# Transposing the memory part into the probability tile and adding it on VectorE, with four smaller edits, in an attention-and-experts kernel

## The chip, the cores and the metric

The kernel runs on one core of one Trainium2 chip. The metric is the device time of one execution in microseconds. All arithmetic is float32 or a split of it.

## The reference

Three layers in a row; only the first is touched, and the last copy of the third.

```python
# B, H, S, D = 4, 8, 576, 64
scores = (q @ k.T) / sqrt(D);  causal mask;  a = softmax(scores);  local = a @ v
phi(x) = where(x > 0, x, exp(x) - 1) + 1
mem_out = (phi(q) @ M_prev) / (phi(q) @ z_prev + 1e-6)
g = sigmoid(beta)
x = g * mem_out + (1 - g) * local          # to (2304, 512)
x = square(relu(x @ w_in)) @ w_out         # d_ff 2048
# then 8 experts, top 2 of them for each token, each relu(x @ w1[e]) @ w2[e], gated and summed
```

## The kernel before

The attention stage works on 16 pairs of heads. Of a pair, both heads lie side by side on the 128 partitions (64 each). The 576 tokens of a pair are four units of queries, `u` = 0 to 3: unit 0 holds two row tiles of 128 queries, units 1 and 2 one each, unit 3 the tail of 64. So there are 64 steps `t`, one for each unit, and the program is written out by hand in a fixed order; each engine takes its instructions in that order. The loop of step `t` issues, for TensorE: `scores(t + 3)` (the products of query and key into one of two double banks, L323 or L353, and the mask, L330), `av(t - 1)` (the products of probabilities and values into bank 7, L412), then `transp(t)` (probabilities turned through banks 4 and 5, L377, L385, L387). VectorE takes the row minimum of `scores(t + 3)` (L334) and copies bank 5 to SBUF (L382, L388); ScalarE makes the exponentials (L339, L358), copies bank 4 (L380, L386) and copies bank 7 into the tile `xT` that the next layer reads (L93, in `put_x`); GpSimd scales the probabilities (L349, L364).

The memory part of a pair is made one pair ahead by `phi_part`: exp of the raw queries on ScalarE (L279), minimum with 1 and a fused maximum-and-add on VectorE (L284, L285), two batches of products with M and z into bank 6 (L291), and a division (L294 to L296) that leaves `mem[n]`, tokens on the partitions, five row tiles. `av` then adds it to the local part inside TensorE: it multiplies the rows of `mem` with an identity into the same bank 7 (L417), two products (one for each head) for each row tile.

`scaled` makes -0.125 times the queries of a pair on ScalarE (L270), into a tile `qs` that the score products read. It is placed by `later(step, ...)`, which runs pieces at the end of a step; so are the four pieces of `phi_part` and the conversion of the first weights of the next layer (`convert`, one part about every four steps, L249 to L258). Copies of activations between two layers (`split_x`) stand in steps 39 to 60.

Everything behind the attention stage (the two dense layers, the routing, the eight experts) is unchanged but for `evac`, which copies an expert's result out of a bank with the gate as a scale (L781 on ScalarE for even tiles, L783 on VectorE for odd ones) and starts an indirect DMA that adds it to the output (L784).

## Time and profile before

| what | value |
|---|---|
| median of 3 runs (lowest, highest) | 1119.62 us (1117.81, 1119.9) |
| the profiled execution's own time | 1117.35 us |
| its span, first to last instruction | 1115.6 us |
| TensorE busy | 1094.4 us, 98% |
| VectorE, ScalarE, GpSimd busy | 591.4, 512.4, 239.0 us |
| attention stage | from the start to about 231 us |

The attention stage is the first fifth of the span. Times in the rows are microseconds from the span's start; an engine's mean is for one instruction in ns. PE is TensorE, PEld its weight loads, DVE VectorE, ACT ScalarE, POOL GpSimd. A float32 product is two records in the trace (two passes), a transposition one.

### The profile page before, as it was taken

The page shows a single profiled execution, that of the slowest core. Times are in us where ns is not written, and L with a number is a line of the kernel's source. Part 1 is how long each engine was busy: PE and PEld are TensorE (multiplying, and loading weights), DVE is VectorE, ACT ScalarE, POOL GpSimd, SP SyncE. Part 2 cuts the span into 40 slices and gives each one's busy share as a digit, 9 for nine tenths or more (in the row PEclk, how much of TensorE's full clock was granted, in tenths as well). Part 3 has the DMA queues.
Part 4 walks back from the last instruction along what each step waited for, and adds up shares of the span by engine and source line. Part 5 has one row for each costly group of instructions (what it writes and reads, how often), then busy time and mean ns, then how long its engine had stood idle before and what let it go on. Part 6 is the DMA issues. An engine that isn't in the chain of part 4 may idle for free. (4 is left out here: it accounts for less than half of the span.)

```text
span 1115.6 us, 19030 instructions
## 1 busy us (share of the span) xinstructions
PE 1094.4 (98%) x7182; PEld 955.5 (86%) x7182; DVE 591.4 (53%) x1484; ACT 512.4 (46%) x1202; POOL 239.0 (21%) x357
## 2 busy tenths in 40 slices
PE   8999999999999999999999999999999999999996
PEld 6777777789999888998988989899999999999995
DVE  6788777669995445434347545444444444342211
ACT  5777777667665334334245533433333333331211
POOL 5566666600000022200202012102020202020202
PEclk9999999999999999999999999999999999999998
DMA  6996532034330011100115508536353545442113
GB/s 193 279 275 212 168 100 86 18 106 126 119 118 19 2 57 57 48 10 11 58 52 153 175 20 225 161 100 147 98 133 105 130 113 125 121 87 37 24 23 46
DMA packets 98278, 115.47 MB, mean 104 GB/s; under 512 B 9984, under 2 KB 67328, under 8 KB 98176
## 3 DMA queue, kind: packets, MB, share of 16 engines
q1 hardware_dynamic: 89664, 94.42, 28.1%
q0 software_dynamic: 8512, 19.74, 8.7%
q8 instruction: 58, 0.95, 0.4%
q14 instruction: 44, 0.36, 0.1%
HBM read 77.80 MB, written 36.33 MB: 102 GB/s over the span
## 5 line engine op out<-in xcount | busy, mean ns | idle before, releaser
L472 PE MATMUL bk<-xsplit,u 128*128 128x384 f32 x1152 | 219.8, 338 | 0.0
L564 PE MATMUL bk<-u,hsplit 128*128 128x512 f32 x864 | 215.2, 393 | 0.0
L773 PE MATMUL bk<-u,hsplit 128*128 128x512 f32 x802 | 213.8, 391 | 0.0
L472 PEld LDWEIGHTS bk<-xsplit,u 128*128 128x128 f32 x1152 | 202.5, 188 | 9.4 <-issue 3.1
L564 PEld LDWEIGHTS bk<-u,hsplit 128*128 128x128 f32 x864 | 160.7, 188 | 29.3
L773 PEld LDWEIGHTS bk<-u,hsplit 128*128 128x128 f32 x802 | 147.3, 188 | 27.0
L764 ACT ACTIVATE hsplit<-bk 128x312 fp32r<-128x312 f32 (+2 forms) x126 | 54.3, 431 | 180.6 <-PE bk L760 180.6
L760 PE MATMUL bk<-xsplit,u 128*128 128x312 f32 (+1 forms) x864 | 134.7, 311 | 1.9 <-ACTq L925 1.9
L760 PEld LDWEIGHTS bk<-xsplit,u 128*128 128x128 f32 x864 | 128.4, 188 | 4.7 <-ACTq L925 2.3
L695 POOL DMA_INDIRECT xs<-x,si x36 | 38.3, 1064 | 410.3 <-DVE runs L688 173.4
L483 ACT ACTIVATE hact<-bk 128x384 f32<-128x384 f32 x96 | 46.6, 486 | 141.1 <-PE bk L472 141.1
L596 DVE TENSOR_TENSOR u<-xT,u 128x512 fp32r<-128x512 f32 x89 | 60.9, 691 | 86.7 <-ACT u L595 85.6
L784 POOL DMA_INDIRECT out_dram<-xT,tk x30 | 47.6, 1587 | 270.1 <-ACT xT L781 263.4
L488 DVE TENSOR_TENSOR hact<-hact 128x384 f32<-128x384 f32 x64 | 35.7, 558 | 124.4 <-ACT hsplit L484 124.4
L595 ACT ACTIVATE u<-xT 128x512 fp32r<-128x512 f32 x89 | 55.6, 628 | 88.6 <-PE bk L773 81.0
L760 PE MATMUL bk<-x2b,u 128*128 128x312 f32 x576 | 87.7, 308 | 0.0
L760 PEld LDWEIGHTS bk<-x2b,u 128*128 128x128 f32 x576 | 83.3, 189 | 0.6
L349 POOL TENSOR_SCALAR P<-P,sm,omg 128x128 f32<-128x128 f32 (+3 forms) x126 | 76.2, 617 | 31.7 <-DVE rd L294 27.8
L765 DVE SCALAR_TENSOR_TENSOR hsplit<-bk,hsplit 128x312 fp32r<-128x312 f32 (+2 forms) x68 | 33.0, 487 | 87.3 <-ACT hsplit L764 87.3
L339 ACT ACTIVATE P<-bk,mx 128x128 f32<-128x128 f32 (+3 forms) x128 | 66.0, 528 | 12.9 <-DVE mx L334 12.7
L412 PE MATMUL bk<-PT,vr 128*64 128x128 f32 (+2 forms) x896 | 59.8, 269 | 0.6 <-ACT PT L380 0.3
L765 DVE SCALAR_TENSOR_TENSOR xsplit<-bk,hsplit 128x312 fp32r<-128x312 f32 (+1 forms) x58 | 27.7, 477 | 60.0 <-ACT hsplit L764 59.5
(188 smaller groups left out, 1464.6 us busy)
## 6 DMA issues: line engine op xcount, KB each, us to landing
xT<-in_moe_w_dram SPq DMA_DIRECT2D x89, 256.0 KB, 3.2
cst<-in_moe_w_in_dram SPq DMA_DIRECT2D x32, 256.0 KB, 2.8
cst<-in_moe_w_out_dram SPq DMA_DIRECT2D x32, 256.0 KB, 2.9
xs<-zero SPq DMA_DIRECT2D x5, 1536.0 KB, 10.7
out_dram<-zero SPq DMA_DIRECT2D x4, 1472.0 KB, 7.4
qr<-in_q_dram SPq DMA_DIRECT2D x16, 352.0 KB, 3.1
xr<-xs SPq DMA_DIRECT2D x7, 774.0 KB, 5.0
vr<-in_v_dram SPq DMA_DIRECT2D x16, 320.0 KB, 3.6
```

What stands on the lines that cost most here:

```text
L339: nc.scalar.activation(pb[:, j * 512 + o:j * 512 + o + w], sp[:, j, o:o + w], AF.Exp, bias=mx[:, x:x + 1], scale=-1.0, accum_out=sm[:, x:x ...
L349: (nc.gpsimd if t or j else nc.vector).tensor_scalar(v, v, sm[:, x:x + 1], omg[:, h0 + j:h0 + j + 1], op0=ALU.mult, op1=ALU.mult)
L412: nc.tensor.matmul(o[j * D:(j + 1) * D, a:e], vv[:k_, c, j, :], pt[:k_, j * step + x:j * step + x + e - a], start=i == 0, stop=False, skip ...
L472: nc.tensor.matmul(hb, l[:, sl], r, start=cc == 0 and n == 0, stop=cc == NCC - 1 and n == 2)
L564: nc.tensor.matmul(bank[y0 + t], l[:, sl], r, start=fc == 0 and n == 0, stop=fc == NFC - 1 and n == 2)
L595: nc.scalar.activation(hi, st, AF.Copy)
L596: eng.tensor_sub(lo, st, hi.bitcast(F32))
L760: nc.tensor.matmul(bank[bk][:, :n_], l[:, cs], r[:, cc, sl], start=cc == 0 and n == 0, stop=cc == NCC - 1 and n == 2)
L764: nc.scalar.activation(hh[:, sl], bank[bk][:, :n_], AF.Relu)
L765: nc.vector.scalar_tensor_tensor(hl[:, sl], bank[bk][:, :n_], 0.0, hh[:, sl].bitcast(F32), op0=ALU.max, op1=ALU.subtract)
L773: nc.tensor.matmul(bank[self.ybank + t], l[:, sl], r, start=fc == 0 and n == 0, stop=fc == NFE - 1 and n == 2)
L784: add = nc.gpsimd.indirect_dma_start(out=out, out_offset=bass.IndirectOffsetOnAxis(ap=self.tok[:n, t:t + 1], axis=0), in_=y, in_offset=Non ...
```

## The change

- The memory part of a row tile is no longer multiplied into bank 7. In `transp` of units 0, 1 and 3 the tile of `mem` is turned by TensorE (one transposition of 128 x 128) into the free columns of the banks that hold the turned probabilities, and comes to SBUF with the copies of these banks, which grow from 384 to 512 columns (for unit 3 from 128 to 256). Unit 1 turns the tiles of units 1 and 2. `put_x` then makes one VectorE addition of bank 7 and that tile, in place of ScalarE's copy. The very first unit (`t` = 0) keeps the old way. The tiles `PT` get three buffers in place of two.
- ScalarE copies bank 5 as well in units 2 and 3, which VectorE did.
- Features: for all pairs but the first, relu(-x) and exp(-that) on ScalarE in place of exp on ScalarE and a minimum on VectorE. In the first pair the minimum stands ahead of the exponential.
- `scaled` runs one step earlier.
- Eight identity products into bank 7 stand between the second and third score products of the program.
- The last copy of the last expert is cut in halves of 256 columns, the first on ScalarE, the second on VectorE.

```diff
--- before.py
+++ after.py
@@ -85,12 +85,17 @@
         return [xsplit[:, (2 * i + j) * NCC * w:(2 * i + j + 1) * NCC * w].rearrange("p (c t) -> p c t", c=NCC)
                 for j in range(2)]
 
-    def put_x(hp, t0, src):
+    def put_x(hp, t0, src, more=None):
+
         n = src.shape[-1]
         while n:
             g, o = divmod(t0, G)
             w = min(n, G - o)
-            nc.scalar.activation(xT[g][:, hp, o:o + w], src[:, :w], AF.Copy)
+            if more is None:
+                nc.scalar.activation(xT[g][:, hp, o:o + w], src[:, :w], AF.Copy)
+            else:
+                nc.vector.tensor_add(xT[g][:, hp, o:o + w], src[:, :w], more[:, :w])
+                more = more[:, w:]
             src, t0, n = src[:, w:], t0 + w, n - w
 
     NE = w1.shape[0]
@@ -276,12 +281,16 @@
         ph = ap2.tile([P, S], F32, name="phi", bufs=2)
         mg = ap2.tile([P, MW], F32, name="mg", bufs=1)
         mem[n] = ap2.tile([P, NB, P], F32, name="mem")
-        nc.scalar.activation(e, qq, AF.Exp)
+        if n:
+            nc.scalar.activation(e, qq, AF.Relu, scale=-1.0)
+            nc.scalar.activation(e, e, AF.Exp, scale=-1.0)
+        else:
+            nc.vector.tensor_scalar_min(e, qq, 0.0)
+            nc.scalar.activation(e, e, AF.Exp)
         nc.gpsimd.tensor_scalar(mg[:, :P], mr_[n % 2][:, :P], gtc[:, n % (H // 2):n % (H // 2) + 1], 1.0,
                                 op0=ALU.mult, op1=ALU.mult)
         nc.gpsimd.tensor_copy(mg[:, P:], mr_[n % 2][:, P:])
         yield
-        nc.vector.tensor_scalar_min(e, e, 1.0)
         nc.vector.scalar_tensor_tensor(ph, qq, 0.0, e, op0=ALU.max, op1=ALU.add)
         yield
         for ts in ((0, 1, 2), (3, 4)):
@@ -364,28 +373,39 @@
             nc.gpsimd.tensor_scalar(pb[:, :S], pb[:, :S], sm[:, :1], omgc[:, h0 // 2:h0 // 2 + 1],
                                     op0=ALU.mult, op1=ALU.mult)
 
+    apart = {}
+
     def transp(t):
         n, u = units[t]
         pb = PB.pop(t)
-        pt = ap3.tile([P, 2 * 512], F32, name="PT", bufs=2)
+        pt = ap3.tile([P, 2 * 512], F32, name="PT", bufs=3)
         PT[t] = pt
         if u < NK - 1:
-            m = sum(w for _, w, _ in tiles(u))
+            turn = t and u < 2
+            m = sum(w for _, w, _ in tiles(u)) + (P if turn else 0)
             blocks = [(0, 0), (1, 1), (2, 2)] if u == 0 else [(c, c) for c in range(u + 2)]
             for j in range(2):
                 for c, x in blocks:
                     nc.tensor.transpose(bank[4 + j][:, x * P:(x + 1) * P], pb[:, j * 512 + c * P:j * 512 + (c + 1) * P], ident)
+                if turn:
+                    nc.tensor.transpose(bank[4 + j][:, 3 * P:], mem[n][:, 2 * u + j, :], ident)
                 dst = pt[:, j * 512:j * 512 + m]
-                if j == 0:
-                    nc.scalar.activation(dst, bank[4][:, :m], AF.Copy)
+                if j == 0 or u == 2:
+                    nc.scalar.activation(dst, bank[4 + j][:, :m], AF.Copy)
                 else:
                     nc.vector.tensor_copy(dst, bank[5][:, :m])
+            if turn:
+                apart[t] = [pt[:, (4 * j + 3) * P:(4 * j + 4) * P] for j in range(2)]
+                if u:
+                    apart[t + 1] = apart[t][1:]
         else:
             for c in range(4):
                 nc.tensor.transpose(bank[4][:, c * P:(c + 1) * P], pb[:, c * P:(c + 1) * P], ident)
             nc.scalar.activation(pt[:, :512], bank[4], AF.Copy)
             nc.tensor.transpose(bank[5][:, :P], pb[:, 4 * P:], ident)
-            nc.vector.tensor_copy(pt[:, 512:512 + P], bank[5][:, :P])
+            nc.tensor.transpose(bank[5][:, P:2 * P], mem[n][:, NB - 1, :], ident)
+            nc.scalar.activation(pt[:, 512:512 + 2 * P], bank[5][:, :2 * P], AF.Copy)
+            apart[t] = [pt[:, 512 + 2 * P - TAIL:512 + 2 * P]]
 
     def av(t):
         n, u = units[t]
@@ -396,27 +416,31 @@
         if u == 0:
             w = 2 * P
             work = [(0, P, 0, 0, w), (1, P, w, P, w)]
-            rows = [(0, 0), (1, P)]
+            rows = [(0, 0), (1, P)] if not t else []
         elif u < NK - 1:
             w = P
             work = [(c, P, c * P, 0, w) for c in range(u + 2)]
-            rows = [(u + 1, 0)]
+            rows = []
         else:
             w = TAIL
             work = [(c, P, c * P, 0, w) for c in range(NB)]
-            rows = [(u + 1, 0)]
+            rows = []
         o = bank[7][:, :w]
         step = TAIL if u == NK - 1 else 512
         for i, (c, k_, x, a, e) in enumerate(work):
             for j in range(2):
                 nc.tensor.matmul(o[j * D:(j + 1) * D, a:e], vv[:k_, c, j, :], pt[:k_, j * step + x:j * step + x + e - a],
-                                 start=i == 0, stop=False, skip_group_check=True)
+                                 start=i == 0, stop=i + 1 == len(work) and not rows, skip_group_check=True)
         for i, (qi, a) in enumerate(rows):
             k_ = min(P, w)
             for j in range(2):
                 nc.tensor.matmul(o[j * D:(j + 1) * D, a:a + k_], mem[n][:, qi, j * D:(j + 1) * D], ident[:, P - k_:],
                                  start=False, stop=i + 1 == len(rows), skip_group_check=True)
-        put_x(hp, b * S + q0, o)
+        if rows:
+            put_x(hp, b * S + q0, o)
+        else:
+            for i, more in enumerate(apart.pop(t)[:len(tiles(u)) if u < NK - 1 else 1]):
+                put_x(hp, b * S + q0 + i * P, o[:, i * P:min(w, (i + 1) * P)], more)
 
     NU = len(units)
     CONV0, CONVR, CONVM = 3, 4.1, 1.9
@@ -430,7 +454,7 @@
         yield
 
     for m in range(1, NPAIR):
-        later(NK * (m - 1) - 1, first(m))
+        later(NK * (m - 1) - 2, first(m))
         gen = phi_part(m)
         for k_ in range(4):
             later(NK * (m - 1) + k_, gen)
@@ -496,8 +520,11 @@
     gates()
     sg = {t: scores(t) for t in range(LEAD)}
     phi0 = phi_part(0)
-    for x in (sg[0], sg[0], sg[1], sg[1], sg[0], sg[0], sg[0], sg[1], sg[2], sg[1], phi0, sg[2], sg[1], phi0, sg[2]):
+    for i, x in enumerate((sg[0], sg[0], sg[1], sg[1], sg[0], sg[0], sg[0], sg[1], sg[2], sg[1], phi0, sg[2], sg[1], phi0, sg[2])):
         next(x, None)
+        if i == 2:
+            for _ in range(8):
+                nc.tensor.matmul(bank[7][:, :P], ident, ident, start=True, stop=True)
     transp(0)
     run_late(-1)
     ahead_of = {}
@@ -777,7 +804,11 @@
             for t in tiles[:self.nt]:
                 n = min(P, WIDE - (self.t0 + t) * P)
                 y = ytile()[:n, :]
-                if t % 2 == 0:
+                if self.e == NE - 1 and t == NT2 - 1:
+                    h = DM // 2
+                    nc.scalar.activation(y[:, :h], bank[self.ybank + t][:n, :h], AF.Copy, scale=self.gate[:n, t:t + 1])
+                    nc.vector.tensor_scalar_mul(y[:, h:], bank[self.ybank + t][:n, h:], self.gate[:n, t:t + 1])
+                elif t % 2 == 0:
                     nc.scalar.activation(y, bank[self.ybank + t][:n, :], AF.Copy, scale=self.gate[:n, t:t + 1])
                 else:
                     nc.vector.tensor_scalar_mul(y, bank[self.ybank + t][:n, :], self.gate[:n, t:t + 1])
```

On TensorE, at the end of a pair (`av` of unit 3 of one pair, `transp` of unit 0 of the next; `bk_64` is bank 7, `bk_61` and `bk_62` are banks 4 and 5, `vr` the values, `ident` the identity). Before:

```order
L412 MATMUL bk_64<-PT,vr_142 64x64 [waits Activation_49]
L412 MATMUL bk_64<-PT,vr_142 64x64 x7
L412 MATMUL bk_64<-PT,vr_142 64x64 [waits DVE_49]
L412 MATMUL bk_64<-PT,vr_142 64x64
L417 MATMUL bk_64<-ident,mem 64x64 x2
L377 MATMUL bk_61<-ident,P 128x128 [waits Pool_49] x2
L377 MATMUL bk_61<-ident,P 128x128
L377 MATMUL bk_62<-ident,P 128x128
L377 MATMUL bk_62<-ident,P 128x128 [waits Pool_49]
```

and now:

```order
L432 MATMUL bk_64<-PT,vr_142 64x64 [waits DVE_49,Activation_49]
L432 MATMUL bk_64<-PT,vr_142 64x64 x7
L432 MATMUL bk_64<-PT,vr_142 64x64 [waits Activation_49]
L432 MATMUL bk_64<-PT,vr_142 64x64
L389 MATMUL bk_61<-ident,P 128x128 [waits Pool_49] x2
L389 MATMUL bk_61<-ident,P 128x128
L391 MATMUL bk_61<-ident,mem 128x128
L389 MATMUL bk_62<-ident,P 128x128
L389 MATMUL bk_62<-ident,P 128x128 [waits Pool_49]
L389 MATMUL bk_62<-ident,P 128x128
L391 MATMUL bk_62<-ident,mem 128x128
```

The two products of `mem` ahead of the transpositions are gone, two transpositions of `mem` stand among the others, and the first product of `av` waits for VectorE as well as for ScalarE.

On VectorE, from the row minima of a unit 0 to the division of the next pair's memory part (`mx` are the minima, `sm` the sums, `rd` the divisors). Before:

```order
L334 TENSOR_REDUCE mx<-bk_68 128x2 [waits PE_49]
L334 TENSOR_REDUCE mx<-bk_68 128x2
L382 COPY PT<-bk_62 128x384 [waits PE_49]
L362 RECIPROCAL sm<-sm 128x1 [waits Pool_49]
L284 TENSOR_SCALAR phe<-phe 128x576 [waits Activation_49]
L285 SCALAR_TENSOR_TENSOR phi<-qr_138,phe 128x576 [waits DMAHW7_49,DVE_49]
L334 TENSOR_REDUCE mx<-bk_69 128x2 [waits PE_49]
L382 COPY PT<-bk_62 128x512 [waits PE_49]
L343 RECIPROCAL sm<-sm 128x4 [waits Pool_49]
L294 TENSOR_SCALAR rd<-bk_63 128x6 [waits PE_49]
L295 RECIPROCAL rd<-rd 128x6 [waits DVE_49]
L296 TENSOR_TENSOR mem<-bk_63,rd 128x384 [waits DVE_49]
```

and now:

```order
L343 TENSOR_REDUCE mx<-bk_68 128x2 [waits PE_49]
L343 TENSOR_REDUCE mx<-bk_68 128x2
L97 TENSOR_TENSOR xT_90<-bk_64,PT 128x128 [waits PE_49,Activation_49]
L97 TENSOR_TENSOR xT_90<-bk_64,PT 128x64 [waits DVE_49]
L97 TENSOR_TENSOR xT_91<-bk_64,PT 128x64
L396 COPY PT<-bk_62 128x512 [waits PE_49]
L371 RECIPROCAL sm<-sm 128x1 [waits Pool_49]
L294 SCALAR_TENSOR_TENSOR phi<-qr_138,phe 128x576 [waits DMAHW7_49,Activation_49]
L343 TENSOR_REDUCE mx<-bk_69 128x2 [waits PE_49]
L97 TENSOR_TENSOR xT_91<-bk_64,PT 128x128 [waits PE_49,Activation_49]
L352 RECIPROCAL sm<-sm 128x4 [waits Pool_49]
L303 TENSOR_SCALAR rd<-bk_63 128x6 [waits PE_49]
```

The minimum on `phe` and a copy of 512 columns went away, additions into `xT` came in behind the minima `mx`, and the first copy is wider. The additions' tiles of 64 are pieces of a tile that crosses the border of an `xT` tile.

On ScalarE, around the scaling of the queries of that same pair. Before:

```order
L339 ACTIVATE P,sm<-bk_69,mx 128x384 [waits DVE_49,Pool_49]
L339 ACTIVATE P,sm<-bk_69,mx 128x384
L93 ACTIVATE xT_93<-bk_64 128x128 [waits PE_49]
L386 ACTIVATE PT<-bk_61 128x512 [waits PE_49,Activation_49]
L339 ACTIVATE P,sm<-bk_68,mx 128x512 [waits DVE_49,Pool_49]
L339 ACTIVATE P,sm<-bk_68,mx 128x512
L270 ACTIVATE qs<-qr_138 128x704 [waits DMAHW5_49]
L93 ACTIVATE xT_93<-bk_64 128x64 [waits PE_49]
L380 ACTIVATE PT<-bk_61 128x384 [waits PE_49,Activation_49]
```

and now:

```order
L348 ACTIVATE P,sm<-bk_69,mx 128x384 [waits DVE_49,Pool_49]
L348 ACTIVATE P,sm<-bk_69,mx 128x384
L275 ACTIVATE qs<-qr_138 128x704 [waits DMAHW5_49]
L404 ACTIVATE PT<-bk_61 128x512 [waits PE_49]
L407 ACTIVATE PT<-bk_62 128x256 [waits PE_49]
L348 ACTIVATE P,sm<-bk_68,mx 128x512 [waits DVE_49,Pool_49]
L348 ACTIVATE P,sm<-bk_68,mx 128x512
L394 ACTIVATE PT<-bk_61 128x512 [waits PE_49,Activation_49]
L367 ACTIVATE Pt_156,sm<-bk_69,mx 128x576 [waits DVE_49,Pool_49]
```

The scaling moved from behind the exponentials of unit 2 to ahead of the copies of the tail's transpositions, the copies into `xT` are gone, and the copy of bank 5 (256 columns) is new.

## Rows read from the trace of the kernel before

**Rows 1.** The page: busy time, share of the span and instructions of each engine

```profile
PE 1094.4 (98%) x7182; PEld 955.5 (86%) x7182; DVE 591.4 (53%) x1484; ACT 512.4 (46%) x1202; POOL 239.0 (21%) x357
```

**Rows 2.** Windows: length, busy time of each engine, granted clock, DMA share, GB/s

```profile
24.00:225.00 201.00, 196.59 (x2141) 149.48 (x2140) 155.49 (x366) 144.30 (x441) 124.09 (x244) 1.00 0.54 164
...
111.25:124.63 13.38, 13.07 (x144) 9.94 (x144) 10.92 (x26) 9.97 (x33) 7.96 (x17) 1.00 0.66 222
```

**Rows 3.** Waits of TensorE, 20 to 235 us: total, times, longest of one

```profile
PE bk L323 <- ACT qs L270: 2.5, 8, 0.3
```

**Rows 4.** Timeline of TensorE: three of the 16 starts of a tail's score products

```profile
54.61 1.13 PE L353 MATMUL bk<-kr,qs 128*128 128x288 f32 x4
...
161.66 1.14 PE L353 MATMUL bk<-kr,qs 128*128 128x288 f32 x4
...
216.63 1.13 PE L353 MATMUL bk<-kr,qs 128*128 128x288 f32 x4
```

**Rows 5.** Timeline of TensorE inside one pair

```profile
111.25 0.93 PE L323 MATMUL bk<-kr,qs 64*128 64x128 f32 x8 [0.31 <-ACT qs L270]
...
113.03 0.61 PE L417 MATMUL bk<-ident,mem 128*64 128x128 f32 x8
113.57 0.88 PE L377 MATMUL bk<-ident,P 128*128 128x128 f32 x6
114.37 0.92 PE L323 MATMUL bk<-kr,qs 64*128 64x384 f32 x4
...
116.35 1.09 PE L377 MATMUL bk<-ident,P 128*128 128x128 f32 x8
117.28 0.83 PE L291 MATMUL bk<-mg,phi 128*128 128x130 f32 x6
```

**Rows 6.** Instructions by line and shape, 0 to 400 us: busy, mean ns, idle

```profile
L417 PEld LDWEIGHTS bk<-ident,mem 128*64 128x64 f32 x320 | 20.1, 137 | 0.0
L382 DVE COPY PT<-bk 128x384 f32<-128x384 f32 x32 | 17.8, 555 | 20.1 <-PE bk L377 20.1
L279 ACT ACTIVATE phe<-qr 128x576 f32<-128x576 f32 x16 | 11.1, 692 | 0.0
L382 DVE COPY PT<-bk 128x512 f32<-128x512 f32 x16 | 10.9, 679 | 3.0 <-PE bk L377 2.8
L296 DVE TENSOR_TENSOR mem<-bk,rd 128x384 f32<-128x384 f32 x16 | 8.9, 557 | 0.5
L284 DVE TENSOR_SCALAR phe<-phe 128x576 f32<-128x576 f32 x16 | 7.1, 447 | 0.0
L296 DVE TENSOR_TENSOR mem<-bk,rd 128x256 f32<-128x256 f32 x16 | 6.8, 424 | 0.6
L388 DVE COPY PT<-bk 128x128 f32<-128x128 f32 x16 | 4.6, 285 | 3.1 <-PE bk L387 3.1
```

**Rows 7.** VectorE's window in one pair, then TensorE's timeline

```profile
115.02:122.40 7.38, 7.17 (x16) 1.00 0.62 210
...
122.60 0.80 PE L412 MATMUL bk<-PT,vr 128*64 128x64 f32 x20
```

**Rows 8.** The start: timeline of TensorE, and a window as in group 2

```profile
9.92 1.26 PE L323 MATMUL bk<-kr,qs 64*128 64x512 f32 x4 [1.92 <-ACT P L339]
...
16.84 0.71 PE L291 MATMUL bk<-mg,phi 128*128 128x130 f32 x4 [1.07 <-DVE mem L296]
...
11.96:16.80 4.84, 3.54 (x16) 2.60 (x14) 4.74 (x10) 3.44 (x9) 2.27 (x5) 0.77 0.33 111
11.00:14.00 3.00, 3.00 (x15) 2.47 (x12) 2.24 (x5) 1.28 (x4) 2.82 (x7) 0.50 0.85 292
```

**Rows 9.** The end: timeline

```profile
1095.31 0.43 ACT L764 ACTIVATE xr<-bk 128x312 fp32r<-128x312 f32 x1 [1.29 <-PE bk L760]
...
1095.77 0.48 DVE L765 SCALAR_TENSOR_TENSOR xr<-bk,xr 128x312 fp32r<-128x312 f32 x1 [1.24 <-ACT xr L764]
...
1105.59 0.69 ACT L781 ACTIVATE xT<-bk,gk 112x512 f32<-112x512 f32 x1 [3.45 <-PE bk L773]
```

## The prediction

> **What bounds the kernel now.** I read the busy times first: TensorE works 98% of the span and the next engine 53% [rows 1]. Only an edit that shortens TensorE's stream, or a wait in it, moves the end. Nearly all edits lie in the attention stage, so I then read that stage by windows: from 24 to 225 us TensorE is busy 196.59 of 201 us at a granted clock of 1.00, that is its upper level of 2.4 GHz, while VectorE has 155.49, ScalarE 144.30 and GpSimd 124.09 [rows 2]. In one pair of heads the numbers are 13.07 of 13.38 us for TensorE, 10.92 for VectorE, 9.97 for ScalarE [rows 2]. So TensorE sets the pace, VectorE has 2.5 us a pair to spare and ScalarE 3.4. The pace is a regular one: a tail's score products start at 54.61 and, eight pairs later, at 161.66, which is 13.38 us a pair; from there to 216.63, four pairs with copies for the next layer among them, it is 13.74 [rows 4]. The waits of TensorE name one repeated loss: the scaled queries come late 8 times, 2.5 us in all [rows 3], 0.31 us in the pair shown [rows 5].
>
> **The memory part.** What goes is two products for each of 80 row tiles (5 in each of 16 pairs), except the two tiles of the very first unit. From the weight loads, 320 records keep TensorE's load side busy 20.1 us [rows 6], 1.26 us a pair. By starts, the eight records of a unit 0 take 113.57 - 113.03 = 0.54 us [rows 5], and part of that is a hand-over to the transpositions, which stays when `av` stands right ahead of them. No row shows it alone. At 0.063 a record it is 0.04; from the transpositions, six of which take 0.80 and would stream in 0.70 at the 0.116 that eight take (0.93 / 8) [rows 5], it is 0.10. The 20 records of a pair take 1.35 at the rate of the 0.54, less four hand-overs 0.95 to 1.19. I take 1.05 us a pair as gone, with 0.95 and 1.26 as ends. What comes is five transpositions a pair, 0.065 us each by the difference of eight and six (0.13 for two), 0.116 by the mean; I take the middle, 0.09, so 0.47 a pair (0.33 to 0.58), since they stand inside groups that have their hand-over already. The net is 1.05 - 0.47 = 0.58 us a pair (0.37 to 0.93), and for 78 of 80 tiles, 15.5 pairs, **-9.0 us** (-5.7 to -14.4).
>
> A transposition is also a question of the clock. The pair in the rows has 20 of them among its products and its granted clock is 1.00 [rows 2]. The Trainium skill says ("TensorE: Matmul & The Clock Gate", Part 4: PE-mode transpose) that a transposition does not count as activity of TensorE as a product does, which speaks against exchanging the one for the other. By the row the sum keeps its -9.0; by the rule the clock could fall, and that is the last of the rivals below.
>
> **The work that moves to VectorE and ScalarE.** The additions into `xT` are new. By the built order there are 54 of 128 columns and 32 of 64. The nearest rows are VectorE's division, which also takes one operand from PSUM and one from SBUF: 557 ns for 384 columns and 424 for 256 [rows 6], so 133 ns for 128 columns, and by the same line 291 ns for 128 and 225 for 64. That is 22.9 us, 1.43 a pair. The wider copies cost 2 x (0.679 - 0.555) = 0.25 [rows 6]. What VectorE loses is the minimum, 0.447, the copy of unit 2, 0.679, and that of unit 3, 0.285 [rows 6]. Sum: 10.92 + 1.43 + 0.25 - 1.41 = 11.2 us a pair. ScalarE gets a second pass over 576 elements, 0.69 [rows 6], and two copies that cost VectorE 0.68 and, at 256 columns, at most 0.56 [rows 6], and 0.25 for wider ones: 9.97 + 2.18 = 12.15 at most, with its copies into `xT` not yet taken off. TensorE's new pair is 13.38 - 0.58 - 0.31 = 12.5. So neither becomes the bound by its sum, but VectorE's slack shrinks from 2.5 to 1.3 us.
>
> With that the new wait counts: the first product of `av` now waits for the addition of the unit before, since both use bank 7. Behind `av` on TensorE stand the transpositions, and all copies wait for these. The addition that is latest is that of unit 2, since ahead of it on VectorE stand the division, a part of the weight conversion and a row minimum of 1024 columns. Before, this stretch runs from 115.02 to 122.40 nearly without a gap, 7.17 us busy, and the next `av` starts at 122.60 [rows 7]. The change takes a minimum (0.447) and a copy (0.679) out and puts two additions (0.58) in, so the stretch shortens by 0.55, and TensorE comes to that `av` about 0.5 earlier. It is a tie, on which I put 0.1 us in each of the 12 pairs that hold a conversion (12 parts, one about every four steps): **+1.0 us**, with 0 and 6 as ends (half a microsecond a pair).
>
> **The scaled queries.** One step earlier, a quarter of 13.38 us, they stand behind the exponentials of unit 1. The tile `qr` has been loaded four steps before even then, and SP's order does not change. The 2.5 us go [rows 3]; next late is the copy of bank 4, which `av` needs only after the score products. **-2.5 us**, with 0 as the other end.
>
> **Passes in the first pause.** TensorE waits 1.92 us until 9.92 for the exponentials that free a bank [rows 8], and right behind, from 11 to 14 us, the granted clock is 0.50, the lower level of 1.2 GHz [rows 8]. Eight identity products, 16 records at the 0.116 us of a transposition, are 1.9 us and just fill the pause; at the lower level they end 1.9 us late. But what the start waits for is VectorE: from 11.96 to 16.80 it is busy 4.74 of 4.84 us, and TensorE's second batch waits 1.07 us for it until 16.84 [rows 8]. The minimum of the first pair only changes places inside that stretch. A faster TensorE gives nothing back there: **0**, from -1.5 (the three microseconds at half pace) to +1.0.
>
> **The last copy.** It starts at 1105.59 and takes 0.69 us [rows 9]. Halves would give 0.26 if both engines read the bank at once, but in the built order VectorE's half waits for ScalarE's. How two such steps run in turn the rows show: 0.43 us on ScalarE, and VectorE starts 0.46 after it and needs 0.48 [rows 9], both for 312 columns; in all 0.94, so 256 columns take some 0.84 by the same shares. **+0.15 us** (-0.26 to +0.25). The Trainium skill gives a reason for such an order ("PSUM — Partial Sum Buffer", PSUM bank collisions raise a hardware error): two engines must not access one bank at once on the same partitions. By it the halves cost 0.15, without it they would give 0.26.
>
> **The sum**, against the profiled execution's own 1117.35 us (1.75 more than its span): -9.0 + 1.0 - 2.5 + 0 + 0.15 = -10.35, so 1107.0. That execution lies 2.3 us under the median of the three runs, 1119.62, and under the lowest, 1117.81. The middle of all four is 1118.7, and from there the change gives about **1108.5 us**.
>
> **Rivals.**
> - *VectorE late at bank 7*, faster but by half. If an addition costs 0.2 us more than by the division's rows, or the stretch of rows 7 keeps its 7.4 us, `av` waits 0.4 to 0.5 in the pairs with a conversion or a copy for the next layer, 15 of them, some 6 us: 1114. For it: the tie above. Against it: the stretch loses more than it gains. 0.17.
> - *More goes than the sum has.* The four last pairs take 0.36 us more each than the regular 13.38 [rows 4]; if a shorter stream and a VectorE without the minimum end these waits too, and the net of the memory part is 0.93, the gain is 14.4 + 2.5 + 1.4: 1101. 0.08.
> - *It is absorbed.* The change does less than it says: TensorE's shorter stream only waits for GpSimd's scaled probabilities, whose order and work stay. Then 1118. Against it: GpSimd is busy 7.96 of 13.38 us [rows 2]. 0.07.
> - *Slower by the additions.* Each `av` waits for an addition behind whatever VectorE still has to do. It decides where the wait passes what TensorE saves, 0.58 + 0.16 (2.5 us over 16) = 0.74 us a pair. With VectorE's sum at 13.8, which an addition of 0.8 us in place of 0.29 would make of it, the pair is 0.4 longer than before: 16 x 0.4, 1125. Against it: no row prices such an operation above 0.56. 0.05.
> - *Slower by the clock.* If the stage's clock fell as at the start, three microseconds at half pace cost 1.5 [rows 8]; one such fall in each pair costs 24 and leaves 1132, and seven falls eat the gain. The rule on transpositions above is the reason it could. Against it: 201 us at 1.00 with 20 transpositions a pair [rows 2]. 0.03.
>
> The forecast itself, 1104.5 to 1112.5, has 0.60. A measurement of this kernel tells about 0.2%, 2.2 us, from no change. Faster is forecast, first and second rival: 0.85; same the third: 0.07; slower the last two: 0.08. The range for 8 in 10 runs from 1102.5 (most of the second rival left out) to 1116.
>
> **What would show it.** The products of `mem` shrink to the first unit's 8 records, and 78 transpositions of `mem` are new; the starts of the tail's products come every 12.4 to 12.7 us; the wait for `qs` is gone; additions of 128 columns take 0.27 to 0.32 us; VectorE is busy some 11.2 us a pair. Wrong would be: a wait of `av` for `xT` among TensorE's longest, above 0.4 us a pair; ScalarE's copies of banks 4 and 5 as what TensorE waits for; a granted clock under 1.00 between 24 and 220 us; or a start that moves by more than 1.5 us.

## Result, and the profile after

The changed kernel takes 1109.49 us (median of four runs, 1108.93 to 1109.99) against 1118.82 (four runs, 1117.81 to 1119.9): a ratio of 0.9917, interval 0.9906 to 0.9929, 9.3 us faster. Its profiled execution took 1109.9 us, 7.45 less than that of before. The page's busy line, as in [rows 1]:

```profile
PE 1090.3 (98%) x6964; PEld 951.2 (86%) x6964; DVE 584.5 (53%) x1524; ACT 521.1 (47%) x1178; POOL 239.5 (22%) x357
```

Windows as in [rows 2], the second one regular pair:

```profile
24.00:218.00 194.00, 192.90 (x1944) 145.75 (x1941) 150.39 (x407) 154.92 (x423) 126.25 (x249) 1.00 0.58 172
92.20:104.76 12.56, 12.56 (x132) 9.48 (x130) 10.33 (x29) 10.56 (x30) 8.07 (x16) 1.00 0.70 222
```

A regular pair is 12.56 us where it was 13.38, TensorE fills it wholly, and the clock stays at 1.00 with 30 transpositions in it. VectorE's share is smaller than before, not larger. All waits of TensorE from 20 to 235 us, as in [rows 3]:

```profile
PE bk L432 <- issue: 0.4, 1, 0.4
PE bk L432 <- ACT PT L394: 0.3, 1, 0.3
PE bk L332 <- DMA kr<-in_k_dram: 0.2, 1, 0.2
```

The wait for `qs` is gone, and no `av` waits for an addition. The new and changed instructions, by line and shape as in [rows 6]; the fused operation of the features (L294) took 1153 ns before at the same shape:

```profile
L391 PEld LDWEIGHTS bk<-ident,mem 128*128 128x128 f32 x62 | 8.8, 141 | 0.0
L396 DVE COPY PT<-bk 128x512 f32<-128x512 f32 x31 | 21.4, 690 | 11.6 <-PE bk L391 11.6
L97 DVE TENSOR_TENSOR xT<-bk,PT 128x128 f32<-128x128 f32 x54 | 14.6, 281 | 2.1 <-PE bk L432 1.7 <-ACT phe L286 0.3
L97 DVE TENSOR_TENSOR xT<-bk,PT 128x64 f32<-128x64 f32 x32 | 6.2, 214 | 0.1
L294 DVE SCALAR_TENSOR_TENSOR phi<-qr,phe 128x576 f32<-128x576 f32 x16 | 12.3, 767 | 0.0
L285 ACT ACTIVATE phe<-qr 128x576 f32<-128x576 f32 x15 | 10.2, 681 | 0.0
```

The starts of the tail's score products, one for each pair as in [rows 4]: the second of 16 before, then the second, the twelfth and the last after.

```profile
27.73 1.14 PE L353 MATMUL bk<-kr,qs 128*128 128x288 f32 x4
```

```profile
29.15 1.13 PE L362 MATMUL bk<-kr,qs 128*128 128x288 f32 x4
...
155.04 1.13 PE L362 MATMUL bk<-kr,qs 128*128 128x288 f32 x4
...
207.93 1.13 PE L362 MATMUL bk<-kr,qs 128*128 128x288 f32 x4
```

They give an account of the stage:

| us | first tail | second tail | next ten pairs | last four pairs |
|---|---|---|---|---|
| before | 12.65 | 27.73 | 133.93 | 54.97 |
| after | 11.95 | 29.15 | 125.89 | 52.89 |

So the 14 pairs behind the second tail give 10.12 us, and the start, though 0.70 earlier at the first tail, is 1.42 late at the second. At the end the last copy loses 0.3. In this execution the clock also fell to 0.50 for some 3 us at the branch behind the first expert (near 703 us). That cost it some 1.2 us: from TensorE's first product behind the branch to the end it took 405.55 us, and 404.36 in e1, which is the same kernel without that fall. e1 and e2 show no fall there, e3 and e4 show one, so it is the execution's and not the change's.

### The profile page after: what moved, and what is told of

The parts are those of the page before. It is cut to its first block, busy times and chain, and to the rows that moved or that the text cites. A ratio compares the mean times of both kernels' runs of the same rounds, so it can differ in the third digit from the quotient of the medians.

```text
span 1108.2 us, 18671 instructions
## 1 busy us (share of the span) xinstructions
PE 1090.3 (98%) x6964; PEld 951.2 (86%) x6964; DVE 584.5 (53%) x1524; ACT 521.1 (47%) x1178; POOL 239.5 (22%) x357
```

## Experiments

All are edits of the changed kernel. "Tail" is the start of the second tail's products, "pair" a regular pair (the commonest of the first nine), "14 pairs" from the second tail to the last; these three are from the profiled execution, the rest from all runs.

| kernel | median us (lowest to highest, runs) | ratio to before, interval | tail | pair | 14 pairs |
|---|---|---|---|---|---|
| after | 1109.49 (1108.93-1109.99, 4) | 0.9917, 0.9906-0.9929 | 29.15 | 12.56 | 178.78 |
| e1 again | 1111.21 (1108.03-1111.52, 5) | 0.9917, 0.9901-0.9932 | 30.60 | 12.56 | 179.00 |
| e2 no passes | 1107.11 (1106.39-1109.31, 4) | 0.9889, 0.9873-0.9905 | 28.00 | 12.56 | 179.10 |
| e3 more passes | 1108.36 (1107.19-1108.62, 4) | 0.9895, 0.988-0.991 | 27.61 | 12.56 | 178.57 |
| e4 whole copy | 1109.68 (1108.36-1111.37, 4) | 0.9908, 0.9893-0.9924 | 29.08 | 12.56 | 178.82 |
| e5 memory apart | 1113.39 (1112.18-1114.63, 6) | 0.9948, 0.9936-0.9961 | 27.79 | 13.00 | 183.89 |
| e6 queries late | 1108.39 (1107.4-1109.93, 5) | 0.991, 0.9897-0.9923 | 27.17 | 12.65 | 179.43 |
| e7 features back | 1112.45 (1110.0-1113.67, 6) | 0.9939, 0.9925-0.9952 | 29.40 | 12.73 | 182.56 |
| e8 copy on VectorE | 1110.6 (1108.06-1112.37, 6) | 0.992, 0.9904-0.9935 | 28.45 | 12.72 | 180.62 |
| e9 queries and features | 1113.64 (1112.01-1115.44, 6) | 0.9946, 0.9931-0.9961 | 29.60 | 12.89 | 183.73 |
| e10 more passes, whole copy | 1106.45 (1106.15-1106.76, 4) | 0.9882, 0.9865-0.9899 | 27.61 | 12.56 | 178.46 |
| e11 no passes, whole copy | 1108.46 (1106.2-1109.34, 5) | 0.9898, 0.9881-0.9915 | 27.62 | 12.56 | 178.74 |
| e12 features and copy | 1119.41 (1117.03-1120.62, 11) | 1.0004, 0.9995-1.0013 | 28.07 | 13.31 | 188.31 |

Runs e1 to e4, e5 to e8, e9 to e11 and e12 were made together, each set beside runs of the kernel before. A start differs from one execution to the next by more than most edits do, so the pair and the 14 pairs are what tells the edits of the pair apart.

### The start and the end: e1 to e4

e1 is the changed kernel itself.

> The changed kernel itself, run beside the next three on one chip, as their yardstick: 0.9917 of the kernel before (1109.5 us), tails of the attention stage every 12.56 us from the third pair on, second tail at 29.15 us.

e2 takes the identity products out.

```diff
-        if i == 2:
-            for _ in range(8):
-                nc.tensor.matmul(bank[7][:, :P], ident, ident, start=True, stop=True)
```

> The changed kernel without the eight identity products in the first pause. My theory: they hold the clock up from 11 to 14 us, where TensorE waits for VectorE anyway, and TensorE then idles from 13.1 to 16.8 us, so that the half pace comes from 16.8 to 21 us, where TensorE sets the pace. Without them the half pace is back at 11 to 14 us, the second tail starts at 27.5 to 28.0 us in place of 29.15, and the kernel is 1.2 to 1.7 us faster than the changed one. The rival, that the late start has another cause (the minimum ahead of the exponential, or the old-style first unit): the second tail stays within 0.3 us of 29.15 or comes later, 0 to 1.5 us slower.

e3 adds passes in the next two gaps, ahead of the first and the second batch of memory products of the first pair.

```diff
+            for _ in range(7):
+                nc.tensor.matmul(bank[7][:, :P], ident, ident, start=True, stop=True)
...
+            for _ in range(4):
+                nc.tensor.matmul(bank[7][:, :P], ident, ident, start=True, stop=True)
```

> The changed kernel with seven more identity products ahead of the first batch of memory products of the first pair and four more ahead of the second batch, so that TensorE is hardly idle between 13 and 16.8 us. My theory (the half pace is what costs): the granted clock stays at 1.00 from 16 to 21 us, the second tail starts 1.2 to 2.0 us before 29.15, and the kernel is 1.0 to 2.0 us faster than the changed one. The rival, that the start is bound by VectorE and ScalarE to the first transpositions of unit 1: same within 0.4 us.

e4 leaves the last copy whole, on ScalarE.

```diff
-                if self.e == NE - 1 and t == NT2 - 1:
...
-                elif t % 2 == 0:
+                if t % 2 == 0:
```

> The changed kernel with its last copy whole on ScalarE. My theory: the halves run one behind the other because they read one bank, 0.98 us in all against 0.69, so the whole copy is 0.3 us faster, and the last indirect DMA starts 0.3 us sooner after the start of the last copy. The rival: the halves cost nothing, same within 0.1 us at that place.

The end first: the last copy and the scatter behind it, in the timeline of the changed kernel and then of e4.

```profile
1098.20 0.47 ACT L809 ACTIVATE xT<-bk,gk 112x256 f32<-112x256 f32 x1 [3.45 <-PE bk L800]
1098.70 0.48 DVE L810 TENSOR_SCALAR xT<-bk,gk 112x256 f32<-112x256 f32 x1 [1.85 <-ACT xT L809]
1099.47 1.48 POOL L815 DMA_INDIRECT out_dram<-xT,tk  x1 [0.79 <-DVE xT L810]
```

```profile
1098.19 0.69 ACT L808 ACTIVATE xT<-bk,gk 112x512 f32<-112x512 f32 x1 [3.45 <-PE bk L800]
1099.15 1.48 POOL L811 DMA_INDIRECT out_dram<-xT,tk  x1 [0.48 <-ACT xT L808]
```

From its start to the scatter the copy takes 1.27 us in halves and 0.96 whole: VectorE's half starts only when ScalarE's is done, so halving costs 0.31. In the time of the whole kernel e4 cannot show it, since its start is as slow as that of after.

The start in TensorE's timeline of the changed kernel, the two batches of memory products of the first pair:

```profile
14.80 0.91 PE L300 MATMUL bk<-mg,phi 128*128 128x130 f32 x6 [1.68 <-DVE phi L294]
16.78 1.15 PE L300 MATMUL bk<-mg,phi 128*128 128x130 f32 x4 [1.07 <-DVE mem L305]
```

Windows of the changed kernel and then of e3 (columns as in [rows 2]):

```profile
11.00:14.00 3.00, 2.12 (x17) 1.40 (x11) 2.27 (x5) 1.03 (x2) 2.82 (x7) 1.00 0.86 296
16.00:18.00 2.00, 1.22 (x6) 0.99 (x6) 0.80 (x4) 1.97 (x5) 0.00 (x0) 0.73 0.03 8
18.00:20.00 2.00, 2.00 (x14) 1.23 (x16) 0.75 (x4) 0.16 (x1) 1.83 (x5) 0.50 0.00 0
```

```profile
11.00:14.00 3.00, 3.00 (x26) 2.44 (x21) 2.27 (x5) 1.00 (x2) 2.82 (x7) 1.00 0.92 317
16.00:18.00 2.00, 1.82 (x16) 1.49 (x16) 1.16 (x6) 1.97 (x5) 0.30 (x1) 1.00 0.04 8
18.00:20.00 2.00, 2.00 (x26) 1.35 (x23) 1.43 (x3) 0.30 (x2) 1.93 (x6) 1.00 0.01 3
```

The half pace that stood at 11 to 14 us before [rows 8] stands at 17 to 20 us in this execution. Before, it fell where VectorE set the pace; now it falls behind these two waits, where TensorE has its whole stream to do: from 18 to 20 us 14 records run where e3 has 26. With passes in the two waits too, it does not come, and the second tail is at 27.61. At the medians e2 and e3 are 2.4 and 1.1 us below the changed kernel, with second tails 1.15 and 1.54 earlier. Neither gain is clear of noise, since both intervals meet that of e1, and e1 shows how far one kernel spreads, 1108.03 to 1111.52: the half pace lasts from 16 to 23 us there, and the second tail is 1.45 later than in the execution above.

### The parts of a pair: e5 to e9, e12

e5 puts the memory part back into bank 7.

```diff
-            turn = t and u < 2
+            turn = False
...
-            nc.tensor.transpose(bank[5][:, P:2 * P], mem[n][:, NB - 1, :], ident)
-            nc.scalar.activation(pt[:, 512:512 + 2 * P], bank[5][:, :2 * P], AF.Copy)
+            nc.scalar.activation(pt[:, 512:512 + P], bank[5][:, :P], AF.Copy)
...
-            rows = []
+            rows = [(u + 1, 0)]
```

> The changed kernel with only the memory part put back: its products again end in bank 7 with the group of `av`, no state is turned, nothing is added by VectorE (in the tail ScalarE copies 128 columns of bank 5 instead of 256). Theory: per regular pair the memory part gives 0.45 us, what is left of the fall from 13.38 to 12.56 us when the wait for the scaled queries (0.37 us) is taken off; so a regular pair of 13.0 us and a time 6 to 8 us above the changed kernel's 1109.5, about 1116. Rival A: the whole 0.82 us per pair is the memory part's and the queries' step gives nothing behind it: pair 13.4, time about 1121. Rival B: VectorE and ScalarE take back what TensorE saves, so that the pair stays at 12.6 and the time within 2 us of 1109.5.

Two starts of the tail's products in e5, a regular pair apart:

```profile
93.39 0.89 PE L362 MATMUL bk<-kr,qs 128*128 128x288 f32 x3
...
106.39 0.41 PE L362 MATMUL bk<-kr,qs 128*128 128x288 f32 x1
```

The pair is 13.00 us, as the theory has it: 0.44 us is the memory part's. The time rises less than expected, 0.9948 against 0.9917 or 3.5 us. In the profiled executions, 1114.27 against 1109.9, two things make it less: the start of e5 kept its clock (second tail 1.36 earlier than after's), and in the last four pairs the memory part gives only 53.26 - 52.89 = 0.37 in all. What ends last in those pairs was not looked into.

e6 puts the scaled queries back one step. (The scaling is ScalarE's, L275, not VectorE's as the expectation says.)

```diff
-        later(NK * (m - 1) - 2, first(m))
+        later(NK * (m - 1) - 1, first(m))
```

> The changed kernel with the scaled queries of a pair again one step later on VectorE; nothing else is different. Theory: TensorE waits 0.3 to 0.4 us for them again in most of the pairs, as it did before in those of 13.38 us: pair 12.9, time 2.5 to 5 us above 1109.5, about 1113. Rival: with the new shorter queue of VectorE (its feature operation takes 767 ns where it took 1153) the queries come in time at either place: pair 12.56, no wait of TensorE for qs, time within 1 us of 1109.5.

The longest wait left in the stage of e6 for the queries, in TensorE's timeline, is in one pair of 14:

```profile
80.79 0.93 PE L332 MATMUL bk<-kr,qs 64*128 64x128 f32 x8 [0.29 <-ACT qs L275]
```

The scaling of the queries on ScalarE, before in the pair that starts at 81.37 and in e6 in the regular pair that starts at 90.50:

```profile
83.66 0.78 ACT L270 ACTIVATE qs<-qr 128x704 f32<-128x704 f32 x1
```

```profile
92.59 0.79 ACT L275 ACTIVATE qs<-qr 128x704 f32<-128x704 f32 x1
```

The theory fell: 12.65 for 12.56, 0.65 us over 14 pairs. The two traces together say why. Measured from the tail's scores, TensorE reaches the scores of unit 0 after 2.75 us with the stream of before (in e5, where nothing holds it up) and after 2.85 now, as two transpositions more stand ahead of them; before, they started after 3.12. The queries, behind the exponentials on ScalarE, end after 2.88 in a regular pair of e6 where they ended after 3.07, because the row minima that these exponentials need come 0.19 earlier from VectorE. Of a stall of 0.37 us that leaves 0.08 or 0.09. So the wait had two cures in this change: without the earlier step VectorE's earlier minima still do most of it. The earlier step alone, in the kernel before, was not run.

e7 gives the features back to one exponential and VectorE's minimum.

```diff
-            nc.scalar.activation(e, qq, AF.Relu, scale=-1.0)
-            nc.scalar.activation(e, e, AF.Exp, scale=-1.0)
+            nc.scalar.activation(e, qq, AF.Exp)
...
+        if n:
+            nc.vector.tensor_scalar_min(e, e, 1.0)
```

> The changed kernel with the features of each pair formed as before: one exponential on ScalarE, then VectorE's minimum, then its fused step; the first pair is left as it is now, and nothing else is different. VectorE gets one more operation of some 0.4 us per pair, ScalarE loses one of 0.68 us. Theory: VectorE's addition to unit 2 now ends 0.2 us ahead of the next `av`, so 0.4 us more of VectorE's work per pair can put that `av` some 0.2 us late: TensorE shows a wait for VectorE at `av`, pair 12.6 to 12.9, time 1 to 4 us above 1109.5. Rival: the features are elsewhere in the pair's order than the addition and VectorE idles between (it waits 12 us in sum for products there), so the pair stays at 12.56 and the time within 1 us.

e8 gives VectorE the copy of bank 5 of unit 2.

```diff
-                if j == 0 or u == 2:
+                if j == 0:
```

> The changed kernel with VectorE again copying bank 5 of unit 2, where ScalarE copies it now; nothing else is different. Theory: that copy of 0.6 to 0.7 us stands on VectorE just ahead of the addition to unit 2, which has 0.2 us to spare before the next `av`; `av` waits 0.4 to 0.5 us for it in each pair: pair 13.0, time 5 to 7 us above 1109.5, about 1115.5. Rival: with ScalarE relieved the copy itself comes earlier, and the addition is no later than now: pair 12.56, time within 1 us of 1109.5.

Both put 0.16 to 0.17 us on a pair: e7 within its theory by pair and time, e8 a third of what was expected. And both by the same chain, which neither theory has. Timelines of GpSimd, VectorE and TensorE in one pair, after first, then e7:

```profile
76.12 2.00 POOL L358 TENSOR_SCALAR P<-P,sm,omg 128x128 f32<-128x128 f32 x4
...
76.39 0.17 DVE L303 TENSOR_SCALAR rd<-bk 128x6 f32<-128x6 f32 x1 [0.85 <-PE bk L300]
...
78.30 0.43 DVE L258 SCALAR_TENSOR_TENSOR ca<-cst,ca 128x256 int32<-128x256 int32 x1
...
80.23 0.28 DVE L97 TENSOR_TENSOR xT<-bk,PT 128x128 f32<-128x128 f32 x1
...
79.64 1.13 PE L362 MATMUL bk<-kr,qs 128*128 128x288 f32 x4
80.61 0.19 PE L363 MATMUL bk<-maskt,identb 128*128 128x64 bf16 x1
80.73 0.80 PE L432 MATMUL bk<-PT,vr 128*64 128x64 f32 x20
```

```profile
77.63 2.01 POOL L359 TENSOR_SCALAR P<-P,sm,omg 128x128 f32<-128x128 f32 x4 [0.46 <-DVE rd L304]
...
79.25 0.66 DVE L258 SCALAR_TENSOR_TENSOR ca<-cst,ca 128x256 int32<-128x256 int32 x1
...
81.42 0.28 DVE L97 TENSOR_TENSOR xT<-bk,PT 128x128 f32<-128x128 f32 x1
...
80.59 1.14 PE L363 MATMUL bk<-kr,qs 128*128 128x288 f32 x4
81.56 0.19 PE L364 MATMUL bk<-maskt,identb 128*128 128x64 bf16 x1
81.85 0.80 PE L433 MATMUL bk<-PT,vr 128*64 128x64 f32 x20
```

In after the addition to unit 2 ends 0.22 us ahead of the `av` that needs bank 7 (80.51, 80.73). In e7 it ends 0.24 later, measured from the start of the tail's scores, and `av` starts 0.17 later, 0.15 us behind the addition's end. The list of waits does not show these 0.17, since by the records' modelled ends only 0.10 us of idle time is left between two of them; the starts do. The 0.24 is one operation of the weight conversion, 0.66 for 0.43 us. The work put back makes VectorE's reciprocal ahead of it a microsecond late, measured to the next tail; GpSimd's scaling of probabilities, which waits for that, starts 0.56 later, and in e7 it ends at 79.64, when VectorE's operation has run since 79.25. In after it ends at 78.12, ahead of that operation. In e8 the same operation takes 0.66 us and the addition ends as late as in e7. The copy put back in e8 does not stand just ahead of the addition, as its theory has it: the division, the conversion and a row minimum stand between.

e9 is e7 and e6 together.

> The changed kernel with both the features formed as before and the scaled queries one step later; the memory part stays turned and added. Apart, the later queries put 0.08 us on a regular pair (12.64 for 12.56) and the older features 0.17 us (12.73). Theory: the two are not a sum. With the older features VectorE's maximum of unit 3, and with it ScalarE's exponentials of unit 3 and the scaling of the queries behind them, come 0.24 us later, and TensorE then waits for the queries until 3.19 us after the tail's scores instead of 2.93: a regular pair of 12.90, wait for qs shown by the profile, time some 3 us above that of the kernel with older features alone if their first pauses agree. Rival: the sum, 12.81 per pair. Rival: the features alone decide and the queries' place costs nothing more, 12.73.

The pair is 12.89, the theory's 12.90 and not the sum of 12.81: with the features as before, the queries' place is worth 0.16 us, twice what e6 showed. The time misses the theory's 3 us: it is 1.2 above e7's, as the 14 pairs are, since only the regular pairs pay and the last four are no longer than in e7 (54.38 against 54.42).

e12 is e7 and e8 together.

> The changed kernel with both the features formed as before (VectorE's minimum, and its fused operation beside GpSimd's scaling) and VectorE's copy of bank 5 of unit 2 back; memory part and queries as changed. Each alone put `av` of the tail 0.17 us later (12.73 for 12.56). Theory: in the changed kernel VectorE idles 0.85 us for TensorE's memory products ahead of the division's first operation (rd); the features back take 0.95 us and the copy 0.65 us of such idle time, so either alone just uses it up, and both together overrun it by 0.6 to 0.7 us, which every later operation of VectorE up to the addition to unit 3 inherits: `av` of the tail waits for VectorE 0.6 us or more in each pair with conversions, a pair of 13.1 to 13.4 us, time 1115 to 1118, as slow as a kernel with the memory part apart or slower. Rival: the two are a sum, 12.9 us per pair, about 1113. Rival: both meet the same limit, 12.73, about 1112.

All of the gain is gone: 13.31 us a pair, 1119.41 us. Pair and wait are the theory's, the time lies 1.4 us above its 1118. The waits of TensorE in e12, then VectorE and TensorE in one pair:

```profile
PE bk L433 <- DVE rd L304: 6.1, 9, 0.7
```

```profile
95.33 0.28 DVE L97 TENSOR_TENSOR xT<-bk,PT 128x128 f32<-128x128 f32 x1
...
94.88 0.19 PE L364 MATMUL bk<-maskt,identb 128*128 128x64 bf16 x1
95.76 0.80 PE L433 MATMUL bk<-PT,vr 128*64 128x64 f32 x20 [0.68 <-DVE rd L304]
```

`av` starts 0.15 us behind the end of the addition. The profile names VectorE's next operation (`rd`), which it puts down as the last one that came. Either piece of work just uses up the 0.85 us that VectorE idles ahead of `rd` in the changed kernel (L303 in the timeline of after above); with both, `rd` comes 0.6 us later, measured to the next tail, and the longer operation of the conversion follows as in e7.

### A better version: e10 and e11

e10 is e3 and e4 together, e11 is e2 and e4 together.

> The changed kernel with passes in every gap of the first pause (7 and 4 identity products more) and the last copy whole on ScalarE. Theory: granted clock 1.00 throughout 11 to 22 us, second tail at 27.6, the last copy 0.3 us shorter; together 1.0 to 2.0 us below the changed kernel's 1109.5, so 1107.5 to 1108.5. Rival: the passes delay the products behind them as much as the clock gives back, and the time stays within 0.5 us of the changed kernel's.

> The changed kernel without any passes in the first pause and with the last copy whole on ScalarE. Theory: second tail at 28.0 with half clock at 11 to 14 us, where VectorE sets the pace, and none behind; the last copy 0.3 us shorter; time 2.0 to 2.7 us below the changed kernel's 1109.5, about 1107. Rival: the gain of leaving out the passes was the luck of its executions, and the time is within 0.5 us of that with more passes.

e10 has the lowest median, 1106.45 us, 3 us below the changed kernel with intervals that do not meet; from e2 and e3 its interval is not apart. Its runs lie within 0.6 us, and each has a mean granted clock of 0.996 or more. e11 misses its expectation: 1108.46, runs from 1106.2 to 1109.34 with clocks from 0.993 to 0.996. Its profiled execution has no half pace in the start, where that of e2 has one at 11 to 14 us. So whether the clock falls in the first pause is not settled by the program alone. Of nine profiled executions with eight passes, five show 0.50 at 18 to 20 us (after, e1, e4, e7, e9; second tail 29.1 to 30.6), e8 a fall at 12 to 16 (28.45), three none (e5, e6, e12; 27.2 to 28.1); of two without passes one falls; of two with passes in every gap none. Two windows, of e6 with eight passes and of e11 with none, where after has 0.50:

```profile
18.00:20.00 2.00, 2.00 (x26) 1.59 (x23) 1.02 (x2) 0.38 (x1) 1.93 (x4) 1.00 0.23 71
```

```profile
18.00:20.00 2.00, 2.00 (x26) 1.34 (x23) 1.44 (x3) 0.31 (x2) 1.93 (x6) 1.00 0.05 11
```

e10 is also 1.9 us below e3, where the last copy explains 0.3; e3's profiled execution has a clock of 0.83 at 698 to 708 us, which fits part of it, and the rest is open.

## Why the prediction was right

- **The time** (1108.5) was right within a microsecond, and that is partly luck, since the terms were off and cancelled: those of the pairs sum to -10.5 with the wait at bank 7, and the 14 pairs gave -10.12, but with some -5 each from the memory part and the rest where the sum has -9.0 and -2.5.
- **Memory part** (-9.0): the mechanism held, the size did not. It measured 0.44 us a regular pair for 0.58. A transposition costs 0.11 us from start to start, not 0.09, and what went is then 0.44 + 0.55 = 0.99, not 1.05. (By its own 0.09 the five are 0.45 and not 0.47, which would have made the forecast gain larger still.) In the last four pairs it gave 0.37 us in all, where the sum had 2.3. From e5 the 14 pairs give 5.1.
- **Scaled queries** (-2.5): the wait went, and the kernel with everything but the memory part (e5) is 188.90 - 183.89 = 5.0 us faster over 14 pairs than before. But that is mostly not the moved step, which is worth 0.65 (e6), or 1.2 with the features as before (e9 against e7); VectorE's lighter load brings the queries earlier as well. The listed 0.31 us was also 0.38 by the pairs, 13.38 - 13.00.
- **Work moved, the wait at bank 7** (+1.0, from 0 to 6): the place was right, the wait was 0. VectorE was given 11.2 us a pair and had 10.33, though the additions took what was said (281 and 214 ns for 291 and 225). Two fused operations are shorter in a regular pair, that of the features 0.74 for 1.26 us and one of the conversion 0.43 for 0.66, which the prediction left at their old lengths. The rival *VectorE late at bank 7* is real, as e12 shows: with two pieces of work left on VectorE, `av` waits 0.68 us in each of nine pairs and nothing is gained.
- **Passes in the first pause** (0, from -1.5 to +1.0): this step failed. The prediction held that the start waits for VectorE and that a clock there gives nothing back, and it looked no further than the second batch, at 16.84 us. In after the passes keep the clock at 1.00 from 11 to 14 us, but the two waits behind them are left, and the half pace comes after these, in the stretch where TensorE sets the pace: +1.42 at the second tail, and +2.9 in e1, above the bound. Five of nine executions with the passes show this and three show no fall, with second tails at 27.2 to 28.1 against 27.73 before. So the start can be late by it, and that the passes make a fall there more likely is not shown: of the kernel before one execution is on record.
- **Last copy** (+0.15): the order was right, the halves cost 0.31, above the bound of 0.25. The reads run in turn as said (0.47 and 0.48 us, 0.03 between them), but 256 columns take as long as the 312 of [rows 9], so 0.98 in all and not 0.84. (In plain proportion to the columns the prediction's 0.94 would have given 0.77; its 0.84 is not worked out.)
- **Slower by the clock**: 1.00 from 24 to 218 us with 30 transpositions a pair, so that rival did not come. (The pair before has 25 and not 20: the prediction counts those of units 0 to 2 and leaves out the five of the tail.) What the rule of the Trainium skill behind it ("TensorE: Matmul & The Clock Gate", Part 4: PE-mode transpose) would do in a stretch of transpositions alone, no run here shows.
- **The other rivals** did not come either: a regular pair fell by 0.82 us with TensorE busy all through, and the last four pairs gave 2.08 us in all (54.97 to 52.89), so what makes them longer than the others did not end.

## What to carry to other kernels

The idle time of an engine, summed over a pair, does not say what an operation moved onto it will cost; what counts is how much of it lies ahead of the place where another engine waits. Here VectorE idles 2.2 us of a 12.56 us pair, and yet either of two pieces of work costs 0.17 us and both together 0.75, nearly the whole gain. So edits that look like extras (features on ScalarE, a copy on ScalarE) can be what the main edit rests on, and they should be tried in pairs as well as alone, since neither their gains nor their losses add. A pass that is to keep TensorE's clock up should be judged by what comes behind the pause as well: with one gap filled the fall came later in five executions of nine, at a place where it costs more, and with all three filled it came in neither of two. One profiled execution does not tell such a fall from luck.

## What the runs showed of the hardware

VectorE's fused operation on the features and GpSimd's scaling of the tail's probabilities (both 128 x 576, in SBUF) lengthen each other, and it is the one that starts second that pays. In the kernel before, in after, then in e7:

```profile
88.45 0.95 POOL L364 TENSOR_SCALAR Pt<-Pt,sm,omgc 128x576 f32<-128x576 f32 x1 [1.70 <-DVE sm L362]
...
88.74 1.26 DVE L285 SCALAR_TENSOR_TENSOR phi<-qr,phe 128x576 f32<-128x576 f32 x1
```

```profile
86.17 0.74 DVE L294 SCALAR_TENSOR_TENSOR phi<-qr,phe 128x576 f32<-128x576 f32 x1
...
86.36 1.26 POOL L373 TENSOR_SCALAR Pt<-Pt,sm,omgc 128x576 f32<-128x576 f32 x1 [1.09 <-DVE sm L371]
```

```profile
87.47 0.95 POOL L374 TENSOR_SCALAR Pt<-Pt,sm,omgc 128x576 f32<-128x576 f32 x1 [1.10 <-DVE sm L372]
...
87.76 1.26 DVE L295 SCALAR_TENSOR_TENSOR phi<-qr,phe 128x576 f32<-128x576 f32 x1
```

VectorE first: 0.74 and 1.26 us. GpSimd first, before and in e7: 0.95, and VectorE 1.26, in e7 ending 0.60 after GpSimd's end at 88.42. So by taking the minimum off VectorE the change made the operation behind it 0.52 us shorter as well, since it now starts ahead of GpSimd's. The Trainium skill states the reason ("SBUF — State Buffer", SBUF: two separate sides): the two engines share a pair of ports, and of a VectorE operation with two inputs in SBUF and a GpSimd operation that reads SBUF the first to start holds it and the other is blocked. The trace agrees in who pays, by these durations. It does not show a block of the whole operation: the second one ends 0.71 us (GpSimd) and 0.60 us (VectorE) after the first, less than the 0.95 and 0.74 that it takes when it starts first.

After and e1 are one program, and TensorE's granted clock differs between their executions: at 0.50 from 17 to 20 us and again for 3 us near 703 us in after, from 16 to 23 us and not near 703 in e1.
